# Gate transposes one step later, three shared PSUM banks, and a new order of the work

## The chip, the cores and the metric

The kernel runs on one core of a Trainium2 chip. The metric is device time in microseconds of the whole program. Three runs of the kernel before gave 551.77, 553.25 and 554.15 us; the median is 553.25.

## The reference

Two blocks follow each other. The first is linear attention with sketched features, for 4 batches, 4 heads, 1088 tokens and 32 columns a head (all float32 on the chip, the sketches S1 and S2 arrive as float64):

```
phi(x) = outer(S1 x, S2 x)            # 8 x 8 = 64 features
kv, z  = sum_s phi(k) v,  sum_s phi(k)
x      = phi(q) kv / (phi(q) z + 1e-6)  # heads side by side: 4 x 1088 x 128
```

The second takes x through 4 attention experts of width 64, of which each token uses the best 2:

```
w, topk = softmax over the 2 best of x @ w_gate
for each expert e:                    # causal attention, 1088 x 1088
    a   = softmax(x wq[e] (x wk[e])^T / 8, causal)
    out += w[e] * (a @ (x wv[e])) @ wo[e]   # only for tokens that chose e
```

## The kernel before

**Preparing a batch.** `prepare(b)` returns a list of pieces, each a cost in us and a function. They turn k and q (`begin`, on VectorE), multiply them by the sketch matrix SKW (`sketch`, tiles kps and qps, copied to kab and qab), build the 64 features (`products`: kp, qp), sum k's features against v (`kvs`), transpose q's features (`turn_features`, tile tq), divide (`numer`, tile num, then VectorE's den and xs), transpose to x (`turn_x`, tile tx), and project: `project_v` (tile vg, values and gate logits), `gate` (a chain of small VectorE operations), `project` (tile qk) and `project_tails` (tile qkt). S arrives as float64 and is split into a high and a low float32 part by some twenty VectorE operations; the sketch matmuls use both, and GpSimd adds the two halves in `products`.

**Attention.** A batch has 17 units: for each pair of 128-query blocks p = 0 to 3, each pair of experts g and each block x of the pair, `scores` (tile sc, matmul and a causal mask added by a second matmul; then VectorE's maximum mx and ScalarE's exponential a), and at the end `scores_last` for the last 64 queries, whose last 64 keys go to two small tiles ext. The exponentials are transposed in groups of four (`turns_of`, tile tp) and copied to aT. After each second unit `close` scales the gate weights by the softmax sums (`gates`: VectorE r, GpSimd rb, two TensorE transposes into tile rt, ScalarE copy rs) and does the first half of the values matmuls (tile av); the second half and the product with rs come a unit later (`rest`), and `output` (tile po, copy ob, store) later still.

**Order.** TensorE's order is written by hand, in the loop from L559 on; the other engines' order is left to the framework, which also adds the waits. Batch 0 is prepared whole before its first unit. Within a batch the pieces that prepare the next batch are fillers: in unit n the loop issues the scores of n, then the transposes of unit n-1 with a share of the fillers between them (`spend`, which pays costs from a running account), a waiting `rest` or `output`, then `close` of the unit before. What is left at the end of a batch is issued at once.

**PSUM.** Eight banks: two tiles of two banks for sc, two banks for tp and ext (`ps_tp`), one for av (`ps_o`), one for every filler, rt and po (`ps_f`). In batch 0's first part the fillers also use the banks of tp and av. A new tile in a bank waits until the readers of the tile before are done. `evacuate` (L72, L74) copies out of PSUM, two of three times on ScalarE, else on VectorE.

Of the kernel before, what the change touches and what calls it, by code (L numbers as in the profile page):

```python
# [19 lines left out]
def kernel(  # L20
# [79 lines left out]
    S_hi = const("S_hi", [128, 32])  # L100
    sketches = [S_hi]
    if S1.dtype == F32:
        nc.vector.memset(S_hi, 0.0)
        for h in range(H):
            for x, s in enumerate((S1, S2)):
                nc.scalar.dma_start(out=S_hi[32 * h + R * x : 32 * h + R * x + R, :], in_=s)
        load(0)
    else:
        raw = const("S_raw", [128, 32, 2], I32)
        nc.vector.memset(raw, 0)  # L110
        for h in range(H):
            for x, s in enumerate((S1, S2)):
                nc.scalar.dma_start(
                    out=raw[32 * h + R * x : 32 * h + R * x + R].rearrange("p d w -> p (d w)"),
                    in_=s.bitcast(I32),
                )
# [3 lines left out]
        S_lo = const("S_lo", [128, 32])  # L120
        sketches.append(S_lo)
# [36 lines left out]
    SKW = const("SKW", [128, len(sketches), 2, H, R])  # L158
    nc.vector.memset(SKW, 0.0)
    for n, s_sb in enumerate(sketches):  # L160
        ST = const(f"ST{n}", [128, 32])
        nc.vector.transpose(ST, s_sb)
        for h in range(H):
            rows = slice(32 * h, 32 * h + 32)
            nc.vector.tensor_copy(SKW[rows, n, :, h, :], ST[rows, 0 : 2 * R].rearrange("d (x r) -> d x r", x=2))  # L165
    NS = len(sketches)
    NB = 4 if NS == 2 else 8

# [34 lines left out]
    def prepare(b):  # L203
# [7 lines left out]
        turns = [0]  # L211
# [148 lines left out]
        kq = nc.vector if first else nc.gpsimd  # L360
        pieces = [(0.0, begin)]
        pieces += [(0.9, lambda j=j: sketch("k", kT, j)) for j in range(0, NJ, NB)]
        pieces += [(0.0, lambda: products("k", kq))]
        pieces += [(0.9, lambda j=j: sketch("q", qT, j)) for j in range(0, NJ, NB)]
        pieces += [(0.0, lambda: products("q", nc.gpsimd))]
        pieces += [(2.0, lambda: (kvs(0), kvs(1)))]
        pieces += [(0.5, lambda y=y: turn_features(y)) for y in range(0, 2 * NJ, 4)]
# [38 lines left out]
    def scores_last(b, qk, z):  # L406
# [217 lines left out]
```

## Time and profile before

| | us |
|---|---|
| median of 3 runs | 553.25 |
| the profiled execution, device time | 555.51 |
| its span, first to last instruction | 553.8 |
| mean granted TensorE clock | 0.929 |
| VectorE busy | 228.8 (41%) |
| GpSimd busy | 71.3 (13%) |

The profile is of one execution. A group's idle time is the time for which its engine did nothing right before instructions of that group, with what ended it. The granted clock is a share of 2.4 GHz.

### The profile page before, as it was taken

Reading aid. Unit: us, or ns where it says so; the run is one execution under the profiler, and the core shown is the slowest. Engines: PE = TensorE matmul, PEld = TensorE weight load, DVE = VectorE, ACT = ScalarE, POOL = GpSimd, SP = SyncE. Lnnn points to the kernel's source line nnn. Section 1 sums busy time; section 2 is a strip of 40 time slices with the busy share of each in tenths; the row PEclk is TensorE's granted clock in tenths of the full one; section 3 lists DMA queues with packets and bytes.
Section 4 is the critical chain, followed back from the end, with each engine's and each line's share of the span. In section 5 each row is a group of like instructions: output and inputs, shape, how many; then the busy total and the mean of one; then the engine's idle time right before and its main releaser. Section 6 shows DMA issues by size and latency. Waiting matters only on the chain.

```text
span 553.8 us, 8147 instructions
## 1 busy us (share of the span) xinstructions
PE 445.4 (80%) x3264; PEld 287.5 (52%) x3264; DVE 228.8 (41%) x486; ACT 230.3 (42%) x556; POOL 71.3 (13%) x99
## 2 busy tenths in 40 slices
PE   0779687889996877968986977887998697999966
PEld 0665445655544654645453664554545364565544
DVE  5424334536532433444645222344273524546431
ACT  0123333455543344244454333444354534556531
POOL 2410450000000261000000044000000000000000
PEclk9978979999997998799999898889799899999979
DMA  7410120000000000000000000000000000000000
GB/s 211 143 50 1 41 81 11 1 11 0 4 9 1 10 4 1 9 1 9 2 11 0 1 13 1 9 2 0 11 1 10 1 1 12 11 11 0 11 1 12
DMA packets 11445, 9.97 MB, mean 18 GB/s; under 512 B 3728, under 2 KB 10384, under 8 KB 11408
## 3 DMA queue, kind: packets, MB, share of 16 engines
q1 hardware_dynamic: 9280, 8.92, 5.5%
q10 hardware_dynamic: 2128, 0.54, 0.5%
q8 instruction: 25, 0.41, 0.3%
q14 instruction: 12, 0.10, 0.1%
HBM read 7.23 MB, written 2.23 MB: 17 GB/s over the span
## 4 chain that ended last, share of the span: by engine, by line
PE 63%; DVE 14%; ACT 10%; issue 5%; POOL 5%; DMA 1%; ACTq 0%; POOLq 0%; DVEq 0%
PE sc L392 14%; PE av L501 12%; PE tp L441 9%; ACT a L378 5%; PE qk L320 5%; PE vg L332 4%; DVE mx L402 3%; PE num L295 3%; PE rt L462 3%; POOL qp L256 3%; PE po L551 2%; PE sc L395 2%; PE av L533 2%; PE kps L244 2%; ACT aT L74 2%
## 5 line engine op out<-in xcount | busy, mean ns | idle before, releaser
L441 PE MATMUL tp<-ident,a 128*128 128x128 f32 (+1 forms) x648 | 106.8, 294 | 21.3 <-ACT a L378 17.0
L378 ACT ACTIVATE a<-sc,mx 128x1024 f32<-128x1024 f32 (+7 forms) x136 | 103.0, 763 | 48.6 <-DVE mx L399 18.0
L74 ACT COPY aT<-tp 128x512 f32<-128x512 f32 (+2 forms) x121 | 64.2, 541 | 131.5 <-PE tp L441 131.0
L441 PEld LDWEIGHTS tp<-ident,a 128*128 128x128 f32 (+1 forms) x648 | 78.8, 151 | 44.5 <-ACT a L378 19.4
L402 DVE TENSOR_REDUCE mx<-sc 128x1 f32<-128x640 f32 (+3 forms) x64 | 62.6, 1020 | 87.4 <-PE sc L395 87.4
L392 PE MATMUL sc<-qkT 64*128 64x512 f32 (+3 forms) x384 | 89.9, 553 | 0.8 <-ACT a L378 0.8
L501 PE MATMUL av<-aT,vt 128*64 128x256 f32 (+1 forms) x640 | 82.0, 388 | 0.0
L457 POOL TENSOR_TENSOR rb<-gw,r 128x256 f32<-128x256 f32 (+1 forms) x36 | 21.2, 589 | 364.6 <-DVE r L454 281.8
L399 DVE TENSOR_REDUCE mx<-sc 128x2 f32<-128x256 f32 (+3 forms) x32 | 26.3, 821 | 80.6 <-PE sc L395 80.5
L392 PEld LDWEIGHTS sc<-qkT 64*128 64x128 f32 x384 | 36.8, 198 | 38.0 <-issue 32.9
L501 PEld LDWEIGHTS av<-aT,vt 128*64 128x64 f32 x640 | 41.9, 142 | 26.9 <-issue 13.1
L72 DVE COPY aT<-tp 128x512 f32<-128x512 f32 (+2 forms) x59 | 37.6, 639 | 28.7 <-PE tp L441 28.4
L462 PE MATMUL rt<-ident,rb 128*128 128x128 f32 x68 | 15.6, 309 | 27.4 <-POOL rb L457 7.3
L320 PE MATMUL qk<-xT,wqk 128*128 128x512 f32 x64 | 35.6, 658 | 1.2 <-DVE vt L72 0.8
L332 PE MATMUL vg<-wvg,xT 128*128 128x260 f32 (+1 forms) x72 | 26.0, 468 | 4.6 <-ACT xT L74 1.4
L464 ACT COPY rs<-rt 128x256 f32<-128x256 f32 (+1 forms) x36 | 13.0, 362 | 39.0 <-PE rt L462 38.6
L551 PE MATMUL po<-wo,yT 128*128 128x128 f32 (+1 forms) x144 | 21.0, 285 | 8.4 <-ACT vt L74 2.4
L378 ACT ACTIVATION_READ_ACCUMULATOR a<-sc,mx 128x1 f32 x136 | 27.3, 201 | 0.0
L462 PEld LDWEIGHTS rt<-ident,rb 128*128 128x128 f32 x68 | 7.6, 149 | 34.1 <-issue 23.9
L286 PE MATMUL tq<-ident,qp 128*128 128x128 f32 x72 | 13.9, 322 | 13.6 <-POOL qp L256 8.5
L395 PEld LDWEIGHTS <-identb 128*128 128x128 bf16 x128 | 7.4, 98 | 31.9 <-issue 30.0
L244 PE MATMUL kps<-SKW,kT 128*128 128x128 f32 x72 | 12.1, 319 | 14.4 <-DVE SKW L165 13.6
(119 smaller groups left out, 433.3 us busy)
## 6 DMA issues: line engine op xcount, KB each, us to landing
kin<-in_k_dram SPq DMA_DIRECT2D x4, 544.0 KB, 4.5
qin<-in_q_dram SPq DMA_DIRECT2D x4, 544.0 KB, 5.9
vin<-in_v_dram SPq DMA_DIRECT2D x16, 128.0 KB, 2.6
out_dram<-ob SPq DMA_DIRECT2D x16, 128.0 KB, 1.8
wqk<-in_moe_wq_dram ACTq DMA_DIRECT2D x1, 128.0 KB
S_raw<-in_S_dram ACTq DMA_DIRECT2D x8, 2.0 KB
wqk<-in_moe_wk_dram ACTq DMA_DIRECT2D x1, 128.0 KB, 3.0
wvg<-in_moe_wv_dram ACTq DMA_DIRECT2D x1, 128.0 KB
```

Source lines behind the costliest of these rows:

```text
L72: nc.vector.tensor_copy(out_, in_)
L74: nc.scalar.copy(out_, in_)
L320: nc.tensor.matmul(t, wt(a), xT[:, 512 * c : 512 * c + 512], start=True, stop=True)
L332: nc.tensor.matmul(t[0:m, 0 : E * HD + E], xT[:, 128 * j : 128 * j + m], wvg, start=True, stop=True)
L378: nc.scalar.activation(out=dst, in_=src, func=ACTF.Exp, bias=mx, accum_out=z)
L392: nc.tensor.matmul(sc[e][:, c0:c1], qk[rows, g, 128 * i : 128 * i + 128], qk[rows, NG + g, c0:c1], start=True, stop=(c1 < n))
L399: nc.vector.tensor_reduce(mx, t[:, :, 0:n], axis=AX.X, op=ALU.max, negate=True)
L402: nc.vector.tensor_reduce(mx[:, e : e + 1], sc[e][:, 0:n], axis=AX.X, op=ALU.max, negate=True)
L441: nc.tensor.transpose(tp[0:nk, k - k0, :], ats[e][:, 128 * j : 128 * j + nk], ident)
L462: nc.tensor.transpose(t[:, 128 * x : 128 * x + 128], rb[:, x], ident)
L501: nc.tensor.matmul(av[HD * e : HD * e + HD, lo:256], vt[:, j, c : c + HD], aT[:, 2 * j + e, lo:256], start=(j == 0), stop=(j == 2 * p + 1))
L551: nc.tensor.matmul(po[0:nq, DM * x : DM * x + DM], yT[:, g, 128 * x : 128 * x + nq], wo_sb[:, g], start=(g == 0), stop=(g == NG - 1))
```

## The change

The separate filler bank goes and `ps_tp` has three banks, which all fillers, tp, rt, po and one ext share; the other ext uses the bank of av. `gates` now returns a function for the transposes, which `rest` calls one unit later. A piece may be empty (`None`), and `spend` issues at most one piece with a cost at a time. S is loaded over two queues, and SKW is built by a product with a mask of ones. The sketch's two halves are added by VectorE as they leave PSUM; in batch 0 the feature products are split between VectorE and GpSimd. In batch 0 the projection of values, the gate and the second half of qk move from the first part into the units; in batches 1 and 2 the second half of qk moves behind the start of the batch. The last batch takes the pairs of blocks from 3 down to 0, with the last unit behind pair 3. The last unit's scores are issued after the transposes of the unit before.

```diff
-    ps_tp = ctx.enter_context(tc.tile_pool(name="ps_tp", bufs=2, space=bass.MemoryType.PSUM))
+    ps_tp = ctx.enter_context(tc.tile_pool(name="ps_tp", bufs=3, space=bass.MemoryType.PSUM))
-    ps_f = ctx.enter_context(tc.tile_pool(name="ps_f", bufs=1, space=bass.MemoryType.PSUM))
...
+    nc.gpsimd.memset(blk, 0.0)
+    for h in range(H):
+        nc.gpsimd.memset(blk[32 * h : 32 * h + 32, h : h + 1], 1.0)
...
+                eng = (nc.scalar, nc.gpsimd)[h % 2]
+                eng.dma_start(out=raw[32 * h + R * x : 32 * h + R * x + R].rearrange("p d w -> p (d w)"),
+                              in_=s.bitcast(I32))
...
-        nc.vector.transpose(ST, s_sb)
-        for h in range(H):
-            rows = slice(32 * h, 32 * h + 32)
-            nc.vector.tensor_copy(SKW[rows, n, :, h, :], ST[rows, 0 : 2 * R].rearrange("d (x r) -> d x r", x=2))
+    nc.vector.transpose(ST.rearrange("p n d -> p (n d)"), S_sum.rearrange("p n d -> p (n d)"))
+    for n in range(NS):
+        nc.vector.tensor_tensor(
+            out=SKW[:, n], in0=ST[:, n, 0 : 2 * R].rearrange("p (x r) -> p x r", x=2)[:, :, None, :].to_broadcast([128, 2, H, R]),
+            in1=blk[:, None, :, None].to_broadcast([128, 2, H, R]), op=ALU.mult)
...
         def bank(name):
-            turns[0] += 1
-            if not first or turns[0] % 4 == 0:
-                return ps_f.tile([128, 512], F32, tag="f", name=name)
-            if turns[0] % 4 == 1:
-                return ps_o.tile([128, 512], F32, tag="o", name=name)
             return ps_tp.tile([128, 512], F32, tag="tp", name=name)
...
-            evacuate(abS[nm][:, j0:j1].rearrange("p j s m -> p (j s m)"), t[:, 0 : w * (j1 - j0)])
+            t = t[:, 0 : w * (j1 - j0)].rearrange("p (j s m) -> p j s m", s=NS, m=64)
+            ab = abS[nm][:, j0:j1]
+            nc.scalar.copy(ab, t[:, :, 0])
             if NS == 2:
-                nc.gpsimd.tensor_tensor(out=t[:, :, 0], in0=t[:, :, 0], in1=t[:, :, 1], op=ALU.add)
+                nc.vector.tensor_tensor(out=ab, in0=ab, in1=t[:, :, 1], op=ALU.add)
...
+        V, G = nc.vector, nc.gpsimd
+        kq, qq = ([V, V, V, G], [V, G, V, G]) if first else ([G] * H, [G] * H)
+        wait = (0.9, None)
+        sk = {nm: [(0.9, lambda j=j, nm=nm, t=t: sketch(nm, t, j)) for j in range(0, NJ, NB)]
+              for nm, t in (("k", kT), ("q", qT))}
+        tq = [(0.5, lambda y=y: turn_features(y)) for y in range(0, 2 * NJ, 4)]
+        nu = [(1.3, lambda g=g: numer(g)) for g in range(NJ // 3)]
+        tx = [(0.4, lambda g=g: turn_x(g)) for g in range(NJ // 3)]
+        vg = [(0.6, lambda j=j: project_v(j)) for j in range(NJ)] + [(0.0, gate)]
+        pr = [[(0.9, lambda a=a, c=c: project(a, c)) for a in (0, 2, 1, 3)] for c in range(2)]
+        pieces = [(0.0, begin)] + sk["k"] + [(0.0, lambda: products("k", kq))]
+        pieces += sk["q"] + [(0.0, lambda: products("q", qq)), wait, (2.0, lambda: (kvs(0), kvs(1))), wait, wait]
+        pieces += tq[0:3] + nu[0:1] + tq[3:4] + nu[1:2] + tq[4:5] + tx[0:1] + nu[2:3] + tx[1:2] + [wait] + tx[2:3]
+        rest = pr[1] + [(0.5, project_tails)]
+        if first:
+            pieces, rest = pieces + pr[0], vg + rest
+        elif b < B - 1:
+            pieces += [wait] + vg + pr[0]
+        else:
+            pieces, rest = pieces + [wait] + vg + pr[0] + rest, []
+        return (qk, vt, gw, gw8), pieces, rest
...
-        ext = [ps_tp.tile([128, 512], F32, tag="tp", name=f"ext{b}_{e}") for e in range(2)]
+        ext = [ps_o.tile([128, 512], F32, tag="o", name=f"ext{b}_0"), ps_tp.tile([128, 512], F32, tag="tp", name=f"ext{b}_1")]
...
-        t = ps_f.tile([128, 512], F32, tag="f", name=f"rt{name}")
-        ...
-        return rs
+        def turn():
+            t = ps_tp.tile([128, 512], F32, tag="tp", name=f"rt{name}")
+            ...
+            return rs
+        return turn
...
         cost, f = fill.popleft()
         debt[0] -= cost
-            f()
+            if f:
+                f()
+            if cost:
+                break
...
-        for p in range((NJ - 1) // 2):
+        for p in range((NJ - 1) // 2) if b < B - 1 else reversed(range((NJ - 1) // 2)):
...
-                    rs = gates(name, z, gw[:, 2 * p : 2 * p + 2, 2 * g : 2 * g + 2], 256)
+                    turn = gates(name, z, gw[:, 2 * p : 2 * p + 2, 2 * g : 2 * g + 2], 256)
                     values(0, p + 1)
                     def rest():
+                        rs = turn()
                         values(p + 1, 2 * p + 2)
...
+            if p == NJ // 2 - 1:
+                yield from last_unit(b, qk, vt, gw8)
...
-        po = ps_f.tile([128, 512], F32, tag="f", name=f"po{b}_{p}")
+        po = ps_tp.tile([128, 512], F32, tag="tp", name=f"po{b}_{p}")
...
+            coming, pieces, rest = prepare(b + 1) if b + 1 < B else (None, [], [])
+            fill.extend(own + pieces)
+            need = len(pieces)
+            share = sum(c for c, _ in fill) / (2 * NJ)
+            for n, (make, turned, close, last) in enumerate(units(b, *now)):
                 ready = list(later)
                 later.clear()
-                gaps = max(len(jobs), 2)
+                if not last:
+                    ats = make()
+                gaps = max(len(turns), 2)
                 for s in range(gaps):
-                    if s < len(jobs):
-                        jobs[s]()
-                    if ready and s:
+                    if ready and s == gaps - 1:
                         ready.pop(0)()
+                    if s < len(turns):
+                        turns[s]()
                     spend(share / gaps)
+                if n == 0 and b == 0:
+                    while len(fill) > need + 5:
+                        spend(1.0)
+                if n == 2 * NJ // 2 - 2:
+                    while len(fill) > need:
+                        spend(1.0)
                 for f in ready:
                     f()
+                if last:
+                    ats = make()
+                    for _ in range(3):
+                        spend(share / 2)
                 if after:
                     after()
                 turns, after = turned(ats), close
...
+            now, own = coming, rest
```

## Rows read from the trace of the kernel before

**Rows 1.** The page: busy us, share of the span, instructions of each engine.
```profile
PE 445.4 (80%) x3264; PEld 287.5 (52%) x3264; DVE 228.8 (41%) x486; ACT 230.3 (42%) x556; POOL 71.3 (13%) x99
```

**Rows 2.** Busy time by stage: stretch, length, PE, PEld, DVE, ACT, POOL, clock, DMA.
```profile
13.63:40.27 26.64, 19.32 (x172) 17.85 (x172) 9.79 (x20) 6.44 (x12) 8.61 (x8) 0.86 0.35 104
40.27:55.45 15.18, 15.18 (x43) 9.28 (x43) 6.14 (x20) 5.30 (x12) 0.00 (x0) 0.80 0.00 1
55.45:179.55 124.10, 100.67 (x699) 62.88 (x698) 54.12 (x108) 54.47 (x134) 18.40 (x21) 0.93 0.06 18
179.55:313.30 133.75, 109.33 (x820) 69.61 (x818) 55.27 (x113) 57.11 (x138) 18.39 (x21) 0.94 0.02 5
313.30:447.30 134.00, 110.58 (x801) 70.02 (x800) 52.40 (x109) 57.49 (x138) 17.16 (x19) 0.91 0.02 5
447.30:553.80 106.50, 90.35 (x740) 57.80 (x738) 43.16 (x80) 48.22 (x121) 5.30 (x9) 0.97 0.03 8
```

**Rows 3.** Busy time in windows of 2 us: first and last slow-clock spell.
```profile
26.00:28.00 2.00, 0.47 (x1) 0.18 (x1) 0.00 (x0) 0.00 (x0) 2.00 (x3) 0.50 0.70 229
...
534.00:536.00 2.00, 1.77 (x8) 1.57 (x8) 0.58 (x4) 0.58 (x1) 0.40 (x1) 0.50 0.00 0
```

**Rows 4.** Groups of TensorE matmuls: busy us, mean ns, idle before, releasers.
```profile
L441 PE MATMUL tp<-ident,a 128*128 128x128 f32 (+1 forms) x648 | 106.8, 294 | 21.3 <-ACT a L378 17.0 <-DVE aT L72 3.0 <-ACT aT L74 1.0
...
L551 PE MATMUL po<-wo,yT 128*128 128x128 f32 (+1 forms) x144 | 21.0, 285 | 8.4 <-ACT vt L74 2.4 <-ACT qkT L74 2.1 <-DVE qkT L72 1.0
...
L462 PE MATMUL rt<-ident,rb 128*128 128x128 f32 x68 | 15.6, 309 | 27.4 <-POOL rb L457 7.3 <-DVE xs L302 3.6 <-ACT qkT L74 2.2
L286 PE MATMUL tq<-ident,qp 128*128 128x128 f32 x72 | 13.9, 322 | 13.6 <-POOL qp L256 8.5 <-ACT qpT L74 2.2 <-ACT kvz L277 1.7
L244 PE MATMUL kps<-SKW,kT 128*128 128x128 f32 x72 | 12.1, 319 | 14.4 <-DVE SKW L165 13.6 <-DVE kab L72 0.8
...
L310 PE MATMUL tx<-ident,xs 128*128 128x128 f32 x36 | 6.2, 281 | 8.6 <-DVE xs L302 4.2 <-ACT xT L74 2.1 <-DVE xT L72 1.9
```

**Rows 5.** Timeline of the start: start us, us, engine, line, operation.
```profile
1.25 5.42 ACTq L113 DMA_DIRECT2D S_raw<-in_S_dram  x8
...
8.39 0.14 DVE L132 TENSOR_SCALAR S_ex<-S_raw 128x32 int32<-128x32 int32 x1
...
11.91 1.66 DVE L165 COPY SKW<-ST 32x16 f32<-32x16 f32 x4
```

**Rows 6.** Groups by form: a two-operand VectorE row, the commonest copy.
```profile
L74 ACT COPY aT<-tp 128x512 f32<-128x512 f32 x95 | 55.0, 587 | 115.2 <-PE tp L441 115.0
...
L346 DVE TENSOR_TENSOR eq<-eq,lower 128x144 f32<-128x144 f32 x4 | 1.2, 300 | 0.0
```

**Rows 7.** Timeline of batch 0's features.
```profile
18.32 1.41 POOL L252 TENSOR_TENSOR kab<-kab 128x576 f32<-128x576 f32 x1 [4.77 <-DVE kab L72]
...
19.76 2.77 DVE L256 TENSOR_TENSOR kp<-kab 128x576 f32<-128x576 f32 x4 [0.32 <-POOL kab L252]
...
24.36 4.57 POOL L256 TENSOR_TENSOR qp<-qab 128x576 f32<-128x576 f32 x4
...
28.98 3.87 PE L286 MATMUL tq<-ident,qp 128*128 128x128 f32 x17 [1.79 <-POOL qp L256]
```

**Rows 8.** Timeline around the last unit of batch 0.
```profile
164.94 0.25 PE L419 MATMUL ext<-cmask,identb 128*64 128x64 bf16 x4
...
167.73 1.11 ACT L378 ACTIVATE a<-sc,mx 128x1024 f32<-128x1024 f32 x1 [4.09 <-DVE mx L426]
...
168.83 0.31 ACT L378 ACTIVATE a<-ext,mx 128x64 f32<-128x64 f32 x1
...
169.28 1.11 PE L441 MATMUL tp<-ident,a 128*128 128x128 f32 x4 [4.09 <-ACT a L378]
```

**Rows 9.** Waits: engine, line and what it waited for; us, times, longest.
```profile
PE tp L441 <- ACT a L378: 17.0, 7, 4.1
```

**Rows 10.** Busy time in a stretch of small units in the last batch.
```profile
460.00:470.00 10.00, 7.22 (x48) 3.50 (x48) 3.67 (x9) 4.32 (x16) 0.61 (x1) 1.00 0.02 4
```

More of the change, by code (lines that the diff above doesn't have):

```diff
@@ L110 @@
         nc.vector.memset(raw, 0)
[L111 to L116, printed above, removed]
+        for x, s in enumerate((S1, S2)):
+            for h in range(H):
+                eng = (nc.scalar, nc.gpsimd)[h % 2]
+                eng.dma_start(out=raw[32 * h + R * x : 32 * h + R * x + R].rearrange("p d w -> p (d w)"),
+                              in_=s.bitcast(I32))
         load(0)
-        S_lo = const("S_lo", [128, 32])
-        sketches.append(S_lo)
+        S_hi, S_lo = S_sum[:, 0], S_sum[:, 1]
         lo, hi = raw[:, :, 0], raw[:, :, 1]
@@ L358, in gate @@
                 nc.vector.tensor_copy(gw8[64 * g : 64 * g + 64], gw[0:64, NJ - 1, 2 * g : 2 * g + 2])
[L360 to L367, printed above, removed]
-        pieces += [(1.3, lambda g=g: numer(g)) for g in range(NJ // 3)]
-        pieces += [(0.4, lambda g=g: turn_x(g)) for g in range(NJ // 3)]
-        pieces += [(0.5, lambda j=j: project_v(j)) for j in range(NJ)]
-        pieces += [(0.0, gate)]
-        pieces += [(0.9, lambda a=a, c=c: project(a, c)) for c in range(2) for a in (0, 2, 1, 3)]
-        pieces += [(0.5, project_tails)]
-        return (qk, vt, gw, gw8), pieces
+        V, G = nc.vector, nc.gpsimd
[19 more added lines that the diff above has]
+        return (qk, vt, gw, gw8), pieces, rest
     def soften(dst, src, mx, z):
@@ L408, in scores_last, with some @@
         sc = [ps_sc.tile([128, 1024], F32, tag="sc", name=f"sc{b}_8_{e}") for e in range(2)]
-        ext = [ps_tp.tile([128, 512], F32, tag="tp", name=f"ext{b}_{e}") for e in range(2)]
-        for c0, c1 in ((0, 512), (512, 1024), (1024, S)):
-            for e in range(2):
-                for g in range(NG):
-                    rows = slice(64 * e, 64 * e + 64)
-                    dst = sc[e][:, c0:c1] if c0 < 1024 else ext[e][:, 0 : c1 - c0]
-                    nc.tensor.matmul(dst[64 * g : 64 * g + 64], qk[rows, g, 1024:], qk[rows, NG + g, c0:c1],
-                                     start=True, stop=(c0 < 1024))
+        ext = [ps_o.tile([128, 512], F32, tag="o", name=f"ext{b}_0"), ps_tp.tile([128, 512], F32, tag="tp", name=f"ext{b}_1")]
+        ext = [t[:, 0:64] for t in ext]
+        def some(dst, e, c0, c1):
+            rows = slice(64 * e, 64 * e + 64)
+            for g in range(NG):
+                nc.tensor.matmul(dst[64 * g : 64 * g + 64], qk[rows, g, 1024:], qk[rows, NG + g, c0:c1],
+                                 start=True, stop=(c0 < 1024))
+        for c in range(0, 1024, 512):
+            for e in range(2):
+                some(sc[e][:, c : c + 512], e, c, c + 512)
+        for e in range(2):
+            some(ext[e], e, 1024, S)
         for e in range(2):
             for g in range(NG):
-                nc.tensor.matmul(ext[e][64 * g : 64 * g + 64, 0:64], identb[:, 0:64], cmask[:, 0:64],
+                nc.tensor.matmul(ext[e][64 * g : 64 * g + 64], identb[:, 0:64], cmask[:, 0:64],
                                  start=False, stop=True)
@@ L459, in gates @@
                                 op=ALU.mult)
-        t = ps_f.tile([128, 512], F32, tag="f", name=f"rt{name}")
-        for x in range(w // 128):
-            nc.tensor.transpose(t[:, 128 * x : 128 * x + 128], rb[:, x], ident)
-        rs = p4.tile([128, 256], F32, tag="rs", name=f"rs{name}", bufs=2)
-        nc.scalar.copy(rs[:, 0:w], t[:, 0:w])
-        return rs
+        def turn():
+            t = ps_tp.tile([128, 512], F32, tag="tp", name=f"rt{name}")
+            for x in range(w // 128):
+                nc.tensor.transpose(t[:, 128 * x : 128 * x + 128], rb[:, x], ident)
+            rs = p4.tile([128, 256], F32, tag="rs", name=f"rs{name}", bufs=2)
+            nc.scalar.copy(rs[:, 0:w], t[:, 0:w])
+            return rs
+        return turn
     fill = collections.deque()
@@ L536, in rest @@
             def rest():
+                rs = turn()
                 half(1)
@@ L584 @@
                 turns, after = turned(ats), close
-            spend(1e9)
-            now = coming
+            while fill:
+                spend(1e9)
+            debt[0] = 0.0
+            now, own = coming, rest
         for f in turns:
```

60 lines of the change are left out of this document (25 added, 35 removed).

## Prediction

> **What bounds the kernel now.** I read the page's busy table first, then busy time by stage, the groups by line with the idle time before them, the waits, and last the timelines of three places. TensorE is the bound: its matmuls cover 445.4 of 553.8 us, so it idles 108.4 us, and no other engine is above 42% [rows 1]. By stage, busy time times granted clock is 19.32 x 0.86 + 15.18 x 0.80 + 100.67 x 0.93 + 109.33 x 0.94 + 110.58 x 0.91 + 90.35 x 0.97 = 413.4 us [rows 2]: that is TensorE's work at the upper level (2.4 GHz). The other 32.0 us of its busy time are what the lower level (1.2 GHz) adds. In windows of 2 us there are 14 such spells, each behind an idle stretch; a window of the first and of the last are shown [rows 3]. One spell costs 32.0 / 14 = 2.3 us. So the span is 413.4 work + 32.0 slow clock + 108.4 idle.
>
> Where the idle lies [rows 4]: rt (gate transposes) 27.4, tp (transposes of the attention tiles) 21.3, tq 13.6, tx 8.6, po 8.4, the first kps 13.6; the rest, 108.4 - 92.9 = 15.5, is many small waits and some 3.1 us behind the last matmul. Of rt's 27.4 only 7.3 are a wait for GpSimd's rb; of tp's 21.3, 17.0 are waits for a softmax. Nearly all the others are waits for ScalarE or VectorE to empty the bank before, the single one of ps_f.
>
> **The change, part by part.** TensorE's instructions stay the same in number and shape, so the 413.4 stays; I go through the idle and then the clock.
>
> *Start.* Before, eight S loads leave the ScalarE queue in 5.42 us, to 6.67; VectorE takes S up 1.7 us later, at 8.39, and the last SKW copies end at 13.57, where the first kps starts [rows 5]. From 8.39 that is 5.2 us. Eight copies (a half is shown as 1.66 with the waits in it, the other took 0.71: 2.4) and a transpose of 0.2 go; two products of 64 columns come, at most 0.30 each by the nearest two-operand row, of 144 columns [rows 6]: 5.2 - 2.6 + 0.6 = 3.2 us. When S lands is open, since half the loads go through GpSimd's queue, from which no row shows a load. From below: four loads at ScalarE's price of 0.68 end at 4.0, VectorE starts at 5.7, first matmul at 8.9, a gain of 4.7. From above: three times that price behind the other queue, so 1.25 + 8.1 + 1.7 = 11.1, first matmul at 14.3, a loss of 0.7. I take 11.4, because the copies' part is sure: -2.2 us. The Trainium skill (DMA: Bandwidth & Descriptors, SWDGE vs HWDGE vs iDMA) says that loads issued from GpSimd have their descriptors computed in software, with a slower setup; no row here shows it, and by it the start would lie on the later side of the 11.4.
>
> *First part of batch 0.* GpSimd's adds (1.41 us for k, as much for q) go; VectorE adds three pieces straight out of PSUM instead. k's products become three on VectorE (2.77 / 4 = 0.7 each) beside one on GpSimd, q's two and two (4.57 / 4 = 1.14 each on GpSimd) [rows 7]. Before, the long run of tq starts 28.98 - 13.63 = 15.4 us after the first kps. After: 36 sketch matmuls 7.1 us (as before), the last q piece copied and added at 8.0, two products on GpSimd 2.3: 10.4. Of the 4.7 us of tq's idle there (1.79 is in [rows 7], 2.91 just before) I keep 1.0. vg, half of qk and the tails, 11.7 of the 15.18 us of the second stage [rows 2], move behind the first scores, where they cover the softmax of the smallest units; as work they are in the 413.4 either way. The Trainium skill (SBUF — State Buffer, Who interferes with whom) says that a VectorE instruction with two SBUF inputs contends with a GpSimd instruction that reads SBUF. No row of before has such products side by side; if they took turns, the k pair would take 2.1 + 1.1 and the q pair 1.4 + 2.3, and the sum would be about 2.5 us longer.
>
> *Gate transposes one step later, three banks.* rt now follows its rb by one unit. In a batch's first units rb stands behind four GpSimd products of 4.6 us together; a unit is about that long, so of the 7.3 us I keep 2. The other 20.1 waited for the one filler bank: now a bank comes back at the third tile, with some 1 us of TensorE work between, against a copy of 0.59 [rows 6]. But the tiles of tp, rt, po and all fillers share the ring, so I keep 3 more. rt: 27.4 -> 5, -22.4. By the same cover tq outside the prologue 8.9 -> 1.5 (empty pieces in the list put other work between products and tq), so tq in all 13.6 -> 2.5, -11.1; po 8.4 -> 2, -6.4; tx 8.6 -> 3, -5.6 (half its wait is VectorE's chain from num to xs, which only the last group still has right before it); the small rest without the end's 3.1, 12.4 -> 4, -8.4. The bounds of each: nothing left, and half left.
>
> *The last unit of a batch.* Before, its two ext tiles hold both tp banks until their softmax ends: the ext matmuls end at 165.19, ext's first exponential at 169.14, and tp waits 4.09 us, to 169.28 [rows 8]; four times, 16 of the 17.0, the longest 4.1 [rows 9]. After, the turns of the unit before come ahead, so tp is free. But ext 0 now sits in ps_o, the single bank of av, and what TensorE has next, fillers apart, is the av of the unit before: it waits for the same exponential as tp did. Two fillers stand before it in batch 1 (qk at about 0.9, 1.8 us), three in batch 2 (2.7), none in 0 and 3. So 4.1 + 2.3 + 1.4 + 4.1 = 11.9 us stay. With 6 us of bank waits (4 before) tp's 21.3 -> 17.9, -3.4. The wait moves rather than goes.
>
> *Large to small in the last batch.* No filler is left there. Before, the small units ran first; 460 to 470 shows 2.78 us idle in 10 [rows 10]. Now eight of them come last, each with 2 to 3 us of TensorE work against a chain scores - max - exponential - transpose of that length: I put 0.5 us on each, 4, and 5 for the last chain (max, two exponentials, gate, transpose, copy, output), of which before ran most under av. Bounds 3 and 15; +9.
>
> Idle: -2.2 - 22.4 - 11.1 - 6.4 - 5.6 - 8.4 - 3.4 + 9 = -50.5. Clock: a spell stays where a long wait stays: four last units, one in the prologue before qk, one in the tail, and two I can't place: 8 x 2.3 = 18.3, -13.7. Span 553.8 - 64.2 = 489.6. The profiled execution took 555.51, 1.7 more than its span, and lies 0.4% above the median 553.25: 491.3 x 553.25 / 555.51 = 489 us.
>
> **Rivals.** (a) *The waits shrink further.* If only the four last units' spells stay (9 us) and idle is 45: 413.4 + 9 + 45 + 1.7, scaled, 467. For: TensorE's work in the loop is bound by no other engine on average [rows 2]. Against: the ext bank.
> (b) *The ring is held by its slowest tile.* Banks come round in order, so num (read three times by VectorE before it is free), kv (held for 72 matmuls) and a copy queued behind two exponentials of 1.1 us [rows 8] stop tp, rt and po alike. If half of rt, po, tx, tq and the rest stays, 16 us come back and three spells with them, 7: 512.
> (c) *Slower.* The same ring, worse than the one bank was: 4 x (45 tp + 36 fillers + 9 rt + 5 po + 1 ext) = 384 tiles go through it. The forecast gain of 64 us is gone when each waits 0.17 us longer than forecast; at 0.2 it is 77 us, 566. For: before, tp had two banks to itself and lost only 4 us to copies. Against: ScalarE is 42% busy.
> (d) *It doesn't do what it says:* rt still waits, for late rb and late copies, and ps_o takes over tp's wait; only start and prologue move, 8 to 10 us: 544.
>
> **How the numbers follow.** Forecast 0.58 (472 to 505 by itself), (a) 0.16, (b) 0.17, (c) 0.04, (d) 0.05. A measurement can't tell less than 0.5%, 2.8 us, from no change; I give that 0.03 out of (d), where the start is lost too. So faster 0.93, same 0.03, slower 0.04. The range, 464 to 524, takes in most of (a) and (b) and leaves out (c), (d) and the edges.
>
> **What would show it.** First kps near 11.4 us; first scores near 36 (55.45 before); rt's idle under 8 us; after each ext an av, not a tp, that waits 1 to 4 us for an exponential; eight slow spells or fewer; the last batch idle at its end and not in its middle. Wrong would be: rt, tp, tq, tx and po with over 45 us of idle together (b or c), the first scores after 42, or a slow clock all through the small units at the end, where their work would double.

## The result and the profile after

| | before | after |
|---|---|---|
| median | 552.85 us (4 runs) | 468.61 us (4 runs) |
| profiled execution, device time | 555.51 | 466.51 |
| its span | 553.8 | 464.7 |
| TensorE busy | 445.4 | 406.0 |
| mean granted clock | 0.929 | 0.986 |

The ratio is 0.8471 [0.8433, 0.8508]. The time lies in the forecast range and 20 us below its centre; the working did not come out term by term, as shown below. Of the ring of two below, three of four executions, the profiled one among them, ran 2% longer than the fourth, at a lower granted clock, so its time is given as a range.

The first four fences are of the changed kernel and answer to [rows 1 to 4]. First the page: busy time, and the granted clock in tenths.

```profile
span 464.7 us, 8178 instructions
PE 406.0 (87%) x3264; PEld 266.7 (57%) x3264; DVE 232.7 (50%) x495; ACT 224.5 (48%) x564; POOL 63.4 (14%) x99
PEclk9999999999998999999999999999999999899997
```

Busy time in stages: up to the first scores, then up to the ext mask matmuls of each of batches 0 to 2, then the rest.

```profile
0.00:39.51 39.51, 19.80 (x180) 16.48 (x180) 21.56 (x54) 8.34 (x17) 12.37 (x35) 1.00 0.52 141
39.51:140.03 100.52, 93.51 (x694) 60.34 (x694) 55.01 (x121) 52.65 (x133) 15.29 (x18) 1.00 0.07 22
140.03:250.00 109.97, 100.14 (x818) 65.66 (x813) 55.52 (x116) 55.46 (x140) 15.60 (x19) 0.98 0.02 6
250.00:359.97 109.97, 102.91 (x831) 67.15 (x826) 53.70 (x116) 56.83 (x143) 14.42 (x17) 1.00 0.02 6
359.97:464.70 104.73, 89.64 (x762) 57.08 (x756) 46.90 (x91) 51.19 (x131) 5.69 (x10) 0.95 0.03 8
```

TensorE is still the bound, and now busy for 87% of the span. In windows of 2 us the sum of busy time times granted clock is 401.4 us, so the lower clock level costs 406.0 - 401.4 = 4.6 us, and 464.7 - 406.0 = 58.7 us are idle. The next fence shows where the lower level comes: a window without work behind batch 0's last scores, the windows after it, and the same place in batch 1.

```profile
142.00:144.00 2.00, 0.00 (x0) 0.00 (x0) 0.83 (x5) 1.18 (x3) 0.00 (x0) 1.00 0.00 0
144.00:146.00 2.00, 1.63 (x8) 0.96 (x10) 0.32 (x2) 1.71 (x7) 0.00 (x0) 0.62 0.01 4
146.00:148.00 2.00, 2.00 (x12) 0.79 (x8) 0.34 (x2) 0.00 (x0) 0.40 (x1) 0.53 0.00 0
148.00:150.00 2.00, 2.00 (x17) 1.57 (x17) 0.42 (x1) 0.82 (x3) 0.00 (x0) 1.00 0.00 0
254.00:256.00 2.00, 1.66 (x16) 1.05 (x16) 0.34 (x3) 2.00 (x7) 0.00 (x0) 1.00 0.00 0
```

After the wait of 4.1 us the granted clock of two windows is 0.62 and 0.53 (a window can hold time at both levels), and then 1.00 again; after the wait of 2.2 us in batch 1 it stays at 1.00. Three such spells are left (144, 404, and the end from 458) of 14 [rows 3]. The one at the end follows no long wait: of the 4 us before it TensorE worked 2.46, and its longest wait there was 0.78 us.

The idle time by group (mean ns of one instruction, then idle time before the group and what ended it):

```profile
L446 PE MATMUL tp<-ident,a 128*128 128x128 f32 (+1 forms) x648 | 98.6, 277 | 5.7 <-DVE vt L71 1.8 <-ACT a L377 1.2 <-ACT qkT L73 0.9
L511 PE MATMUL av<-aT,vt 128*64 128x256 f32 (+1 forms) x640 | 80.6, 381 | 13.1 <-ACT a L377 11.6 <-DVE aT L71 1.4
L325 PE MATMUL vg<-wvg,xT 128*128 128x260 f32 (+1 forms) x72 | 21.9, 400 | 4.8 <-DVE aT L71 2.2 <-DVE vt L71 1.8 <-ACT aT L73 0.7
L567 PE MATMUL po<-wo,yT 128*128 128x128 f32 (+1 forms) x144 | 21.7, 293 | 2.3 <-DVE aT L71 1.1 <-ACT aT L73 0.7 <-ACT vt L73 0.5
L469 PE MATMUL rt<-ident,rb 128*128 128x128 f32 x68 | 13.7, 279 | 5.5 <-DVE aT L71 2.4 <-ACT aT L73 1.8 <-DVE den L294 0.6
L236 PE MATMUL kps<-SKW,kT 128*128 128x128 f32 x72 | 12.1, 320 | 14.2 <-DVE SKW L163 14.2
L279 PE MATMUL tq<-ident,qp 128*128 128x128 f32 x72 | 11.2, 276 | 3.1 <-DVE kT L223 1.4 <-ACT qpT L73 1.0 <-ACT aT L73 0.7
L303 PE MATMUL tx<-ident,xs 128*128 128x128 f32 x36 | 6.0, 275 | 0.9 <-DVE xs L295 0.9
```

Against [rows 4], rt falls from 27.4 to 5.5, tp from 21.3 to 5.7 and tq from 13.6 to 3.1; new is av with 13.1, of which 11.6 are waits for an exponential. Before, av had none:

```profile
L501 PE MATMUL av<-aT,vt 128*64 128x256 f32 (+1 forms) x640 | 82.0, 388 | 0.0
```

The timeline shows that these are the four last units:

```profile
140.03 0.25 PE L424 MATMUL ext<-cmask,identb 128*64 128x64 bf16 x4
144.37 3.63 PE L511 MATMUL av<-aT,vt 128*64 128x256 f32 x16 [4.09 <-ACT a L377]
254.34 1.95 PE L511 MATMUL av<-aT,vt 128*64 128x256 f32 x16 [2.17 <-ACT a L377]
364.29 1.95 PE L511 MATMUL av<-aT,vt 128*64 128x256 f32 x16 [1.23 <-ACT a L377]
403.77 1.48 PE L511 MATMUL av<-aT,vt 128*64 128x256 f32 x6 [4.09 <-ACT a L377]
```

The wait of [rows 8] is still there and merely sits before av. The same 16 av matmuls take 3.63 us after the long wait and 1.95 after the shorter ones: that is the lower clock. The start came later than before, not earlier:

```profile
1.24 1.69 ACTq L117 DMA_DIRECT2D S_raw<-in_S_dram  x4
1.94 2.24 POOL L117 DMA_DIRECT2D S_raw<-in_S_dram  x4
8.78 0.18 DVE L133 TENSOR_SCALAR S_ex<-S_raw 128x32 int32<-128x32 int32 x1 [1.52 <-DMA wo<-in_moe_wo_dram]
9.53 1.30 DVE L224 STREAM_TRANSPOSE qT<-qin 128x1088 f32<-128x1088 f32 x1
11.11 1.05 POOL L218 COPY vp<-vin 128x1024 f32<-128x1024 f32 x1 [5.34 <-DMA vtl<-in_v_dram]
11.14 1.06 DVE L136 TENSOR_TENSOR S_sg<-S_sg,S_ex 128x32 int32<-128x32 int32 x1
14.24 4.14 PE L236 MATMUL kps<-SKW,kT 128*128 128x128 f32 x18 [14.24 <-DVE SKW L163]
19.05 3.08 DVE L249 TENSOR_TENSOR kp<-kab 128x576 f32<-128x576 f32 x3
19.10 1.74 POOL L249 TENSOR_TENSOR kp<-kab 128x576 f32<-128x576 f32 x1 [6.71 <-DVE kab L242]
26.59 1.39 PE L279 MATMUL tq<-ident,qp 128*128 128x128 f32 x11 [1.35 <-DVE kT L223]
```

VectorE stands still for 1.52 us until S is there (8.78; 8.39 in [rows 5]), then has the transpose of q in the middle of the S chain, and one operation of the chain takes 1.06 us beside a GpSimd copy of the same length. What releases the wait at 8.78 is named as a load of wo, which the operation doesn't read; its input S_raw is the load to look at. For GpSimd's four loads the trace shows the time from issue to landing (KB each, median us):

```profile
S_raw<-in_S_dram POOLq DMA_DIRECT2D x4, 2.0 KB, 5.1
```

The last of them is issued at 3.7, and 3.7 + 5.1 = 8.8 is when VectorE goes on.

### The profile page after: what moved, and what is told of

It is laid out like the page before. It is cut to its first block, busy times and chain, and to the rows that moved or that the text cites. A ratio compares the mean times of both kernels' runs of the same rounds, so it can differ in the third digit from the quotient of the medians.

```text
span 464.7 us, 8178 instructions
## 1 busy us (share of the span) xinstructions
PE 406.0 (87%) x3264; PEld 266.7 (57%) x3264; DVE 232.7 (50%) x495; ACT 224.5 (48%) x564; POOL 63.4 (14%) x99
## 4 chain that ended last, share of the span: by engine, by line
PE 68%; DVE 16%; ACT 9%; issue 3%; DMA 2%; POOL 1%; ACTq 0%; DVEq 0%
PE sc L391 16%; PE av L511 15%; PE tp L446 10%; DVE mx L401 6%; ACT a L377 5%; PE qk L313 4%; PE po L567 3%; PE num L288 3%; PE sc L394 3%; PE av L548 2%; DVE aT L71 2%; PE vg L325 2%; DVE mx L429 2%; PE kps L236 2%; PE rt L469 2%
## 5 line engine op out<-in xcount | busy, mean ns | idle before, releaser
L73 ACT COPY aT<-tp 128x512 f32<-128x512 f32 (+1 forms) x119 | 63.5, 542 | 127.6 <-PE tp L446 127.5
L377 ACT ACTIVATE a<-sc,mx 128x1024 f32<-128x1024 f32 (+7 forms) x136 | 103.0, 763 | 36.8 <-DVE mx L431 14.2
L446 PE MATMUL tp<-ident,a 128*128 128x128 f32 (+1 forms) x648 | 98.6, 277 | 5.7 <-DVE vt L71 1.8
L511 PE MATMUL av<-aT,vt 128*64 128x256 f32 (+1 forms) x640 | 80.6, 381 | 13.1 <-ACT a L377 11.6
L446 PEld LDWEIGHTS tp<-ident,a 128*128 128x128 f32 (+1 forms) x648 | 70.8, 141 | 22.4 <-issue 7.4
L391 PE MATMUL sc<-qkT 64*128 64x512 f32 (+3 forms) x384 | 82.6, 518 | 0.0
L391 PEld LDWEIGHTS sc<-qkT 64*128 64x128 f32 x384 | 33.1, 185 | 36.3 <-issue 31.4
L313 PE MATMUL qk<-xT,wqk 128*128 128x512 f32 x64 | 32.4, 603 | 0.8 <-ACT xT L73 0.8
L377 ACT ACTIVATION_READ_ACCUMULATOR a<-sc,mx 128x1 f32 x136 | 27.4, 201 | 0.0
L325 PE MATMUL vg<-wvg,xT 128*128 128x260 f32 (+1 forms) x72 | 21.9, 400 | 4.8 <-DVE aT L71 2.2
L236 PE MATMUL kps<-SKW,kT 128*128 128x128 f32 x72 | 12.1, 320 | 14.2 <-DVE SKW L163 14.2
L521 DVE TENSOR_TENSOR yT<-av,rs 128x256 f32<-128x256 f32 x32 | 13.4, 420 | 21.1 <-PE av L511 20.9
L567 PEld LDWEIGHTS po<-wo,yT 128*128 128x128 f32 (+1 forms) x144 | 18.2, 192 | 6.3 <-DVE aT L71 1.9
L236 PEld LDWEIGHTS kps<-SKW,kT 128*128 128x128 f32 x72 | 10.6, 226 | 15.1 <-DVE SKW L163 14.2
L469 PE MATMUL rt<-ident,rb 128*128 128x128 f32 x68 | 13.7, 279 | 5.5 <-DVE aT L71 2.4
```

The costliest lines, as they stand in the source:

```text
L73: nc.scalar.copy(out_, in_)
L236: nc.tensor.matmul(t[:, w * (j - j0) : w * (j - j0) + w], xT_[:, 128 * j : 128 * j + 128], SKW.rearrange("p s x h r -> p (s x h r)"), star ...
L313: nc.tensor.matmul(t, wt(a), xT[:, 512 * c : 512 * c + 512], start=True, stop=True)
L325: nc.tensor.matmul(t[0:m, 0 : E * HD + E], xT[:, 128 * j : 128 * j + m], wvg, start=True, stop=True)
L377: nc.scalar.activation(out=dst, in_=src, func=ACTF.Exp, bias=mx, accum_out=z)
L391: nc.tensor.matmul(sc[e][:, c0:c1], qk[rows, g, 128 * i : 128 * i + 128], qk[rows, NG + g, c0:c1], start=True, stop=(c1 < n))
```

## The experiments

"Median" is of 4 runs beside the kernel before on the same chip, unless another number is given. "Work" is busy time times granted clock, "slow" the rest of busy time, "idle" the span less busy time, each of one profiled execution.

**The ring of three banks undone, all else of the change kept.** tp gets two banks back; rt, po and the fillers share the third alone.

```diff
-    ps_tp = ... bufs=3
+    ps_tp = ... bufs=2
+    ps_f = ... bufs=1     # rt, po, and every filler once the units run
```

> The changed kernel with the three shared banks undone in the units: tp has two banks, fillers, rt and po one of their own (batch 0's first part uses all three in turn). The turns of the order, the pacing and the later gate transposes stay. Theory of the forecast: the one bank cost rt, po, tq, tx, vg most of their 60 us of idle, so 25 to 45 us come back: 495 to 515, with rt, po, vg, tq idle for copies. Rival: the pacing (at most one filler between two transposes) and the later gates already give the bank time to be emptied: under 480.

Median 557.53 (10 runs), ratio to before 1.0067 [1.0019, 1.0115]: nothing of the gain is left, and both expectations, 495 to 515 and under 480, were too low. tp keeps 9.0 us of idle time; these groups, in the single bank, have what the change had taken away:

```profile
L320 PE MATMUL qk<-xT,wqk 128*128 128x512 f32 x64 | 37.3, 675 | 8.8 <-ACT qkT L75 3.7 <-DVE qkT L73 2.8 <-ACT ob L75 0.9
L332 PE MATMUL vg<-wvg,xT 128*128 128x260 f32 (+1 forms) x72 | 26.8, 457 | 13.5 <-ACT vt L75 7.7 <-DVE vt L73 5.7
L574 PE MATMUL po<-wo,yT 128*128 128x128 f32 (+1 forms) x144 | 24.1, 314 | 7.9 <-ACT qkT L75 2.6 <-ACT kvz L277 1.1 <-DVE vt L73 1.0
L476 PE MATMUL rt<-ident,rb 128*128 128x128 f32 x68 | 14.3, 287 | 25.9 <-DVE qab L249 4.7 <-DVE r L465 4.2 <-DVE kab L249 3.3
```

rt, already one unit later here, idles 25.9 us (27.4 in [rows 4]); 8.0 of them end with VectorE's adds into qab and kab, which empty a filler tile out of the single bank, and vg waits for the copies vt. So without the ring the later step does not shorten rt's wait.

**Three banks alone, on the kernel before.**

```diff
-    ps_tp = ... bufs=2
-    ps_f = ... bufs=1
+    ps_tp = ... bufs=3    # all fillers, rt, po, tp and both ext
```

> The kernel before (552.9 us) with one part of the change alone: no filler bank, ps_tp has three banks, and all fillers, tp, rt, po and both ext tiles share them. Order, gates, first part and last batch are as before. Theory A (the single filler bank was nearly all of it, as the undone part showed: 557 us without the three banks): idle falls from 108 to some 65 us, half of the slow-clock spells go, and the time is 475 to 495 us. Theory B (the three banks only pay together with the pacing and the later gates, since in the old order fillers follow each other): over 515 us.

486.97, ratio 0.8822 [0.8781, 0.8862]: 66 of the 84 us come with this edit alone, as theory A had it. Idle is 59.9, slow 18.9, work 406.2. Its longest waits (us in total, times, longest):

```profile
PE kps L238 <- DVE SKW L164: 12.3, 1, 12.3
PE rt L456 <- POOL rb L451: 10.8, 6, 4.5
PE tq L280 <- POOL qp L250: 10.5, 6, 2.9
```

Behind the start 47.6 us of idle time remain, and 21.3 of them are these waits for GpSimd's results.

**A ring of two.** In the changed kernel:

```diff
-    ps_tp = ... bufs=3
+    ps_tp = ... bufs=2
```

> The changed kernel with two shared banks in place of three; the eighth bank stays unused. It tells apart what counts: that the tiles share a ring (a bank comes back at the second tile at the earliest, not at the next), or that there are three. Theory A (the distance to reuse counts: at least one other tile's work between): 480 to 505 us, waits of 0.2 to 0.5 us spread over tp, rt, po and fillers. Theory B (a ring of two is held by its slowest tile, and no bank is better than two with one kept for fillers): 530 to 570 us.

Median 524.47 (514.92 to 524.68), without an interval; it lies between the ranges of the two theories. The profile shows the place, tp's idle time:

```profile
L446 PE MATMUL tp<-ident,a 128*128 128x128 f32 (+1 forms) x648 | 104.1, 284 | 22.5 <-ACT aT L73 6.8 <-DVE aT L71 5.7 <-ACT qpT L73 2.1
```

Of the 84 us, 28 to 38 are left: with two banks in the ring each tile waits for the copy of the last but one. The time of the forecast's rival (b), 512, is near this kernel and not near the changed one.

**The gate transposes at once**, as before, in the changed kernel:

```diff
-    turn = gates(...)     # rest(): rs = turn()
+    rs = gates(...)()     # in close()
```

> The changed kernel (468.6 us) with one part undone: the gate transposes stand again at the head of close, right behind the scaling on GpSimd, in the three shared banks. Theory of the forecast: of rt's 27.4 us of idle before, 20 were the one filler bank and only 7.3 the wait for GpSimd, so the step later is worth 5 to 10 us: 474 to 479, with rt idle 10 to 15 us, mostly released by GpSimd's rb. Rival: the step is the main part, since rb is always late when nothing else is: rt idle over 20 us and 485 to 495 us.

467.93, ratio 0.8431 [0.8349, 0.8513]: no difference, where 474 to 479 or 485 to 495 were expected. rt now waits 5.7 us for rb (idle 8.9 in all), and av's wait for the exponential falls from 11.6 to 8.3 in exchange. One wait covers the other.

**All fillers of a share at once**, and no empty pieces:

```diff
             if f:
                 f()
-            if cost:
-                break
```

> The changed kernel with the pacing undone: no empty pieces, and several fillers may follow each other at one place again. It asks for the 18 us between the three banks alone (487.0) and the whole change (468.6), where idle was the same (60 and 59 us) but slow clock 18.9 against 4.6. Theory A (the empty pieces keep tq and rt off GpSimd's products, 21 us of waits with the banks alone, and so the clock up): waits for GpSimd come back by a half, 3 spells become 6 to 8, 474 to 482 us. Theory B (the pacing is not it, GpSimd's load is): 466 to 471.

468.14, ratio 0.8476 [0.8428, 0.8523]: no difference, in the range of theory B.

**The adds back on GpSimd**, the halves copied out by `evacuate` as before:

```diff
-            nc.scalar.copy(ab, t[:, :, 0])
-                nc.vector.tensor_tensor(out=ab, in0=ab, in1=t[:, :, 1], op=ALU.add)
+            evacuate(abS[nm]..., t...)     # products: GpSimd adds the halves
```

> The changed kernel with the fused adds undone: both halves of the sketches are copied out and GpSimd adds them (1.4 us, twice a batch) ahead of its products; everything else stays, the split of batch 0's products too. Theory A (pacing is what took GpSimd off the path): the two batches' loops hide it and only the prologue is 2 to 3 us longer: 470 to 473 us. Theory B (GpSimd's load was it): tq and rt wait for GpSimd again, 10 us and more of idle with slow spells, 478 to 486.

473.72, ratio 0.8589 [0.8517, 0.8662]: 5 us, and the intervals don't meet; this is theory A, 0.7 us above its range. The span is 4.2 us longer, and the first scores come 3.8 later (43.34 against 39.51). In this kernel the adds cost their 4 to 5 us nearly all in batch 0's first part.

**Three parts on the kernel before**: the ring of three, the adds on VectorE, the gate transposes one unit later.

```diff
 # the kernel with three banks alone, and
+            nc.scalar.copy(ab, t[:, :, 0])
+                nc.vector.tensor_tensor(out=ab, in0=ab, in1=t[:, :, 1], op=ALU.add)
+            turn = gates(...)     # rest(): rs = turn()
```

> The kernel before with three parts of the change: all of tp, rt, po and the fillers in one ring of three banks, the adds taken from GpSimd (VectorE adds out of PSUM) and the gate transposes one unit later. With the banks alone it took 487.0, and the whole change takes 468.6; of the 18 us between them the adds explain 5. In the banks-alone run TensorE waits 10.8 us for GpSimd's rb and 10.5 for GpSimd's qp. Theory A (these waits, and the clock spells and extra busy time behind them, are what remains): rt <- rb falls below 3 us, tq <- qp below 8, slow clock from 18.9 to 10 or less, and the time is 470 to 475. Rival B (pacing and placement of the fillers, each worth nothing when undone alone beside the others, carry it together): the named waits fall but others come up, time 479 to 483. Rival C (nothing of it): 487.

465.06 (6 runs), ratio 0.8364 [0.8315, 0.8414]: theory A, and further than it said. These three parts are at least as fast as the whole change, so what the others add on top of them can't be told from nothing. Slow is 9.6, idle 49.9, work 404.4. First scores are at 52.18 (52.81 with the banks alone), so the 22 us come out of the units: rt has lost its wait for GpSimd (10.8 to 0.7 us), tq half of it (10.5 to 4.7).

```profile
L459 PE MATMUL rt<-ident,rb 128*128 128x128 f32 x68 | 13.7, 279 | 4.2 <-ACT qkT L73 1.4 <-ACT xT L73 1.2 <-POOL rb L452 0.7
L281 PE MATMUL tq<-ident,qp 128*128 128x128 f32 x72 | 12.5, 306 | 5.3 <-POOL qp L251 4.7 <-ACT qpT L73 0.5
```

The later step, worth nothing in the changed kernel, may be what takes away rt's wait here, where fillers come in bursts and GpSimd's products lie right ahead of rb; the lighter load of GpSimd may be it too. Which of the two parts brings how much here was not run.

**Small tiles first in the last batch**, as before:

```diff
-        for p in range((NJ - 1) // 2) if b < B - 1 else reversed(range((NJ - 1) // 2)):
+        for p in range((NJ - 1) // 2):
```

> The changed kernel with the last batch in the order of the others, small tiles to large. The forecast booked the new order as a loss of 9 us of idle, so by it 460 to 464. Rival: the small units at the end hardly wait (in the trace of after they show under 3 us), while the old order ends with the last unit, whose exponentials and 18 transposes nothing covers: 473 to 480, with a long wait and a slow clock in the last 25 us.

469.75, ratio 0.8452 [0.8378, 0.8526]: no difference that can be told, and neither the 460 to 464 nor the 473 to 480 that were expected.

**Batch 0's first part whole**: values, gate and the second half of qk ahead of the first scores again.

```diff
-            pieces, rest = pieces + pr[0], vg + rest
+            pieces, rest = pieces + vg + pr[0] + rest, []
```

> The changed kernel with batch 0 prepared whole ahead of its first unit, as before the change (values, gate and the second half of qk go back there). Forecast: as work it is the same on TensorE, the move only covers small units: 470 to 473. Rival: the cover of the first units is worth more, since they have nothing else until the next batch's sketches come: 476 to 482, with idle and a slow clock between 45 and 75 us.

464.11, ratio 0.8365 [0.8302, 0.8427], below both expectations, and the interval doesn't meet the changed kernel's: the shortening gains nothing, and by the medians it costs 4 us. The first scores come 10 us later (49.52). The profiled executions, 466.15 and 466.51 us, are alike and can't show the 4 us, so their cause stays open. One difference is in them: a qk now stands ahead of the first last unit's av, which waits 2.15 us instead of 4.09 and has no spell behind it. But in batch 1 the same wait as in the changed kernel, 2.17 us, now has one, and the 16 av matmuls take 3.63 us, not 1.95:

```profile
250.78 3.63 PE L511 MATMUL av<-aT,vt 128*64 128x256 f32 x16 [2.17 <-ACT a L377]
```

**Both ext tiles in the shared ring**:

```diff
-        ext = [ps_o.tile(..., tag="o", ...), ps_tp.tile(..., tag="tp", ...)]
+        ext = [ps_tp.tile(..., tag="tp", ...) for e in range(2)]
```

> The changed kernel with both ext tiles in the shared banks instead of one in av's bank. The four waits of av for ext's exponential (11.6 us in the trace of after) then have no cause. Forecast's step (av waits for the bank alone): av's waits go, but the next scores wait for sc, which the same exponentials hold until 3.5 us after ext, so 1 to 2 us of each long wait move there: 464 to 467 us, and the slow clock at 144 and 404 us goes. Rival: the wait moves whole (to sc or, since two of three banks are held, to fillers and transposes): 468 to 472.

464.08, ratio 0.8395 [0.8372, 0.8419]: 4.5 us as forecast, and the intervals don't meet. av's wait for the exponential is gone, and smaller ones come in its place, 4.3 us of sc and 2.0 and 1.2 of two fillers, qk and qkt: 7.5 for 11.6.

```profile
L391 PE MATMUL sc<-qkT 64*128 64x512 f32 (+3 forms) x384 | 83.7, 518 | 4.3 <-ACT a L377 4.3
L511 PE MATMUL av<-aT,vt 128*64 128x256 f32 (+1 forms) x640 | 78.4, 373 | 1.5 <-DVE aT L71 1.4
```

**All S loads on ScalarE's queue, batch 0's products all on VectorE**:

```diff
-                eng = (nc.scalar, nc.gpsimd)[h % 2]
+                eng = nc.scalar
-        kq, qq = ([V, V, V, G], [V, G, V, G]) if first else ([G] * H, [G] * H)
+        kq, qq = ([V, V, V, V], [V, V, V, V]) if first else ([G] * H, [G] * H)
```

> The changed kernel with two edits of the first part undone: all eight S loads from ScalarE's queue, and batch 0's feature products all on VectorE (no GpSimd beside it). Start: in the trace of after the S chain starts at 8.78, later than before (8.39), and one of its operations takes 1.06 us beside a GpSimd copy, so if the GpSimd half of the loads was the late one, the first kps comes at 12.5 to 13.5 instead of 14.24; rival: VectorE's own order (k and q transposes inside the chain) sets it, and it stays at 14. Products: beside GpSimd three took 3.08 us and two took 2.44 on VectorE (1.0 and 1.2 each against 0.69 before); by contention, four alone take 2.8 each time and tq starts no later than now. Together 466 to 469 us.

Before the change only k's products were on VectorE, q's on GpSimd, so this is not the old kernel's split. 466.30, ratio 0.8425 [0.84, 0.8449]. The time alone can't tell 2 us here; the timeline can:

```profile
1.25 5.20 ACTq L117 DMA_DIRECT2D S_raw<-in_S_dram  x8
8.06 0.14 DVE L133 TENSOR_SCALAR S_ex<-S_raw 128x32 int32<-128x32 int32 x1
9.14 0.19 DVE L136 TENSOR_TENSOR S_sg<-S_sg,S_ex 128x32 int32<-128x32 int32 x1
11.40 4.21 PE L236 MATMUL kps<-SKW,kT 128*128 128x128 f32 x18 [11.40 <-DVE SKW L163]
17.26 2.72 DVE L249 TENSOR_TENSOR kp<-kab 128x576 f32<-128x576 f32 x4
24.48 1.42 PE L279 MATMUL tq<-ident,qp 128*128 128x128 f32 x11 [1.47 <-DVE qp L249]
```

Eight loads on one queue let VectorE start at 8.06 without a wait, 0.72 us sooner than four beside four; both transposes are done by then, S_sg takes 0.19, and the first kps starts at 11.40, before either expectation (12.5 to 13.5, or 14). The first scores gain only 2.1 us (37.42) of these 2.8. From the first kps to the long run of tq it now takes 24.48 - 11.40 = 13.08 us, against 26.59 - 14.24 = 12.35 in the changed kernel: so the loads gain, and the products on VectorE alone, with a transpose of the next batch's k (1.24 us) that VectorE now does ahead of k's, lose 0.7. The loads without the products were not run.

**What pays, together**: batch 0 whole, ext in the ring, S loads on ScalarE, products on VectorE, as in the three diffs above. By the timeline just read the last of the four is no gain.

> The changed kernel with four of its edits taken back or altered as the runs pointed: batch 0 prepared whole (464.1 alone), both ext tiles in the shared banks (464.1 alone), S loaded from ScalarE's queue and batch 0's products on VectorE (466.3 alone). If the three gains are in different places they add: 468.6 - 4.5 - 4.5 - 2.3 = 457, so 455 to 460. If the first two share the slow clock at the first last unit (144 us), 460 to 463.

458.31 (457.38 to 458.57), ratio 0.8297 [0.825, 0.8343], 2% below the change, and the intervals don't meet. Slow is 3.4, in one spell, and idle 50.6.

## Why the prediction came out as it did

The direction and the main cause were right: most of rt's and po's waits and half of tx's were for banks, and the ring took them away; tp's moved to av. The forecast of all idle time, 57.9 us, met 58.7, in part by luck: the start came 2.8 us above its term, tx 2.1 and the rest 2.2 below theirs. The time fell 24.9 us below the forecast span of 489.6 by two terms that were mis-sized, 13.7 and 12.0, less 0.8 of idle.

*Slow clock, 18.3 forecast, 4.6 measured.* The step "a spell stays where a long wait stays" counted eight. Three are left, of 1.5 us each and not 2.3. Of the four last units only the two with waits of 4.09 us have a spell; those of 2.17 and 1.23 have none. There is none in the prologue either; the one in the tail came. The length of a wait alone does not decide it: with batch 0's first part whole the same 2.17 us is followed by a spell, and with ext in the ring a wait of 1.21 us is, while two of 2.04 us in the same run are not. What decides it stays open. Rival (a), which left four, had this nearer, but its 45 us of idle is not what brought 467.

*Work, 413.4 forecast to stay, 401.4 measured.* That busy time times clock is a constant of the instructions was the assumption that failed. In 2-us windows the kernel before has 412.6 (the other 0.8 lies between the two ways of summing) with 108 waits of TensorE, here called gaps, and the changed one 401.4 with 56: 11.2 / 52 = 0.2 us a gap. The runs fall into two groups: with 48 to 59 gaps (eleven kernels) 397 to 406, with 108 to 115 gaps (three, the ring of two among them) 411 to 417. A cause that would fit: one transpose takes 277 ns by itself, but 16 in a row with nothing to wait for take 2.04 us, 128 ns each, so each gap exposes about 150 ns that otherwise overlap. The ends of matmuls are modelled in the profile, so part of it may be the model's. No run changed the number of gaps alone, so this stays an argument from counts; within the first group the gaps don't order the work (48 gaps go with 404.4, 49 with 397.2).

Idle, by the forecast's own terms:

- *Ring:* rt 5 forecast, 5.5 measured; po 2 and 2.3; tq 2.5 and 3.1; tx 3 and 0.9. Right in size, but "one step later" had little part in rt's fall beside the other parts (own bank: 25.9; at once: 8.9 and the same time). tq's fall has another cause than the ring, with which alone it idles 10.5 us, all behind GpSimd's qp. In the changed kernel neither the empty pieces undone (1.9) nor the adds (4.8, of which 3.1 behind qp, in batch 0) brings it back, so which part it is stays open.
- *Last unit:* 11.9 us of av waits forecast as 4.1 + 2.3 + 1.4 + 4.1, measured as 4.09 + 2.17 + 1.23 + 4.09 = 11.6. The chain through av's bank was read rightly, and the run with ext in the ring shows it by taking the wait away. With the bank waits, 17.9 against tp's 5.7 and av's 13.1.
- *Start:* 11.4 forecast (8.39 + 3.2 would be 11.6), 14.2 measured. The copies' saving was there: with all loads on ScalarE the chain takes 11.40 - 8.06 = 3.34 us, 3.2 by the forecast. The split loads took it back. 14.24 - 11.40 = 2.84 is 0.72 for S's later landing, some 1.3 for q's transpose, which fell into the gap that this opened in VectorE's order, and 0.87 for S_sg beside the GpSimd copy (1.06 against 0.19). The bound from above, 14.3, held it by luck: it had VectorE start at 11.1 and the chain at 3.2 us, and the trace has 8.78 and 5.46.
- *Rest:* 16.1 forecast (4 small, 9 for the last batch, 3.1 behind the last matmul), 13.9 measured. The 9 was too much: from 408 us to the last matmul's end at 461.34 TensorE idles 3.5 us in all. The 4 was too little: vg alone has 4.8.
- *First part of batch 0:* the long run of tq starts 26.59 - 14.24 = 12.35 us after kps (10.4 forecast). The last add to q ends 8.7 us after kps (8.0 forecast), and q's products 3.5 us behind it (2.3 forecast). First scores come at 39.5 (36 forecast, with a start 2.8 earlier). That the moved work stays work was right: with the first part whole the scores come 10 us later, and work (401.5) and span (464.4) are the same.
- *Rival (b):* half of the waits that it names is some 17 us by [rows 4], not 16; nothing hangs on it.

On the start, the Trainium skill (DMA: Bandwidth & Descriptors, SWDGE vs HWDGE vs iDMA) says that GpSimd's loads get their descriptors from software, with a slower setup. The trace agrees in sign: four issues take 2.24 us on GpSimd and 1.69 on ScalarE, and with all eight on ScalarE S lands at least 0.72 us sooner.

On the products, the Trainium skill (SBUF — State Buffer, Who interferes with whom) says that VectorE's second SBUF port is GpSimd's, under an exclusive lock. The trace agrees: S_sg, with two SBUF inputs, starts 0.03 us behind the GpSimd copy and ends 0.04 behind it. Of k's three products on VectorE two take 0.75 us and one 1.73 (shortest, median and longest, in ns):

```profile
L249 DVE TENSOR_TENSOR kp<-kab x3: 746/759/1733, 19.0 to 21.4; 128x576 f32<-128x576 f32 x3
```

GpSimd's own beside them takes 1.74. So the split of k's products (3.08 us, 3.2 if they took turns) gained nothing over VectorE alone (2.72). q's products took 3.5 us (3.7 in turns), but VectorE first did a transpose of the next batch's k, 1.23 us, so they don't show turns. The forecast's other sum, 2.5 us longer for taking turns, was nearer: 12.9 against 12.35 measured and 10.4 forecast.

## What to carry to other kernels

When many short producers wait for one PSUM bank, let them and the others share a ring before anything in the order of the work is touched: here the ring gave 66 of 84 us, and the same reordering without it gave nothing. Waits cover each other, so undo each part alone and also build up from the old kernel: the later gate step was worth nothing when taken out of the changed kernel, while with the adds, put into the old one beside the ring, it made 22 us. Where TensorE is the bound, count its gaps as well as their sum: closing them went with 28 us less of slow clock and, as far as the counts tell, some 11 us less of busy time.

## What the runs showed of the hardware

- In the changed kernel a wait of 2.17 us left TensorE's granted clock at 1.00, and a wait of 4.09 us was followed by two windows of 2 us at 0.62 and 0.53; the 16 matmuls behind it took 3.63 us, 1.95 otherwise. With batch 0's first part whole the same wait of 2.17 us was followed by windows at 0.71 and 0.50 and the same 3.63 us, and with ext in the ring a wait of 1.21 us was followed by windows down to 0.50 while two of 2.04 us were not: the length of a wait alone does not tell.
- A 128x32 VectorE operation with two SBUF inputs grew from 0.19 to 1.06 us beside a GpSimd copy of 1.05 us. On GpSimd's side the cost is there too: its kp product took 1.74 us (1.18 in the median of its thirteen).
- Eight small loads split over ScalarE's and GpSimd's queues landed at least 0.72 us later than all eight on ScalarE's; the four on GpSimd's took 5.1 us from issue to landing.
